# Gate/up products from the first 128 rows on, with all gate/up weights resident, loads on two queues and contiguous fold outputs

## The chip, the cores and the metric

The kernel runs on one core of a Trainium2 chip. Such a core has a matrix engine (TensorE, "PE" in the profile, with its weight loads listed apart as "PEld"), a vector engine (VectorE, "DVE"), a scalar engine (ScalarE, "ACT"), a pool engine that does nothing here, and a sync engine ("SP") whose queue starts the transfers between device memory and the core's on-chip memory. Each engine runs its own instructions strictly in the order in which they were written down; engines wait for each other through semaphores. The metric is the time of one execution in microseconds of the device, as a median over runs.

## The reference

The input `x` has 2048 rows of 640 numbers. It is normalised over its rows (layer norm), and three things are added: `x` itself, a spectral filter A and a gated product B of the normalised rows.

```python
def _A_ref(x, w_r, w_i):
    X = rfft2(x.astype(float32), axes=(-2, -1))
    X = X * (w_r + 1j * w_i)
    return irfft2(X, s=(S, D), axes=(-2, -1)).astype(bfloat16)

def _B_ref(x, w_gate, w_up, w_down):
    g = einsum("bsd,df->bsf", x, w_gate)      # 640 -> 1536
    u = einsum("bsd,df->bsf", x, w_up)        # 640 -> 1536
    return einsum("bsf,fd->bsd", g * u, w_down)   # 1536 -> 640

xn = _layernorm(x)
return x + _A_ref(xn, A_w_r, A_w_i) + _B_ref(xn, B_w_gate, B_w_up, B_w_down)
```

## The kernel before

The 2048 rows are held as 16 blocks of 128. All work is cut into tasks, each a handful of instructions on one engine, with a name that is used below:

- **Normalisation of block b** (DVE): two `bn_stats` (L716, L717), `bn_aggr` (L722), subtract the mean (L744), add epsilon (L729), a square root on ACT (L733), the reciprocal (L737) and the multiplication (L749). Blocks are handled in groups (`_LN_GROUPS`): two single ones, then pairs.
- **T0_b** (PE, L757): five transposes that bring the normalised block into the tile `XT`, whose copy out of PSUM runs on ACT or DVE (`eT0`, L671 or L672).
- **GU** (PE, L836): the gate and up products of one of 12 column groups `ft` of 128 columns with one stretch of 256 rows: ten products of 128x256 into one PSUM bank. `eG` (L671) copies the bank to the small ring `GBF` (three slots), and `H` (DVE, L851) multiplies gate by up into `HT`. There are 96 such units.
- **L1_b, L2_b** (DVE, L778/L779 and L788/L789): a block's row is folded twice, so that the transform over the 640 columns can run on quarters of it. L1 makes sum and difference of mirrored halves, L2 folds those once more into `F`. L2 writes every fourth element, since the four quarters lie interleaved in `F` (`p (r d g) -> p r g d`).
- **R_b** (PE, L798): five products on the folded block; `eR` copies them to `U`, on ACT.
- **D_t, C_t, WM_t, CB_t, IA_t, IB_t** for 16 values t: the transform over columns and rows (PE, L881/L885 and L906 to L909), the multiplication with the filter (DVE, L920, with its combination L929/L930) and the first inverse products (PE, L939, L956). The filter rows for t are loaded into a ring of four slots `W`.
- **I_a, U1_a, U2_a** for 16 blocks a: the rest of the inverse transform (PE L979/L983, ACT, DVE L998/L999 and L1006/L1007).
- **ACC_a_h** (PE, L1024/L1026): 12 products with `w_down` and one with the inverse transform for half of an output block, 32 in all; `FIN` (DVE, L1033) adds `x`, and SP stores the half block.

The order on each engine comes from a planner, `_Sched.plan` (L151). It simulates the engines with a duration for each task, a fixed delay between engines and a simple model of the transfers, and at each step takes, among the tasks whose inputs are planned, the one that can start first, with a preference for low `prio` numbers within a slack. What it writes down is fixed: at run time an engine that waits for one task does not go on to the next. Idle PE time up to `filler_deadline` is planned with dummy products (`fill`, L687/L688), and 56 more of them (`warm`, L698) open the program.

The gate and up weights have 12 column groups, of which the tile `GW` holds eight (`_NGW = 8`). GU therefore runs in two passes (`_FT_GROUPS`): first groups 0 to 7 over all eight stretches of 256 rows, then groups 8 to 11 over all of them, whose weights are loaded into the slots of groups 0 to 3 when the last product on those is done. All transfers are started by SP.

Of the kernel before, what the change touches and what calls it, by code (L numbers as in the profile page):

```python
# [10 lines left out]
_XLAT = 130.0  # L11
_SLAT = {"pe": 0.0, "act": 70.0, "dve": 70.0, "pool": 100.0, "sp": 0.0}
_DMA_BW = 300.0
_DMA_LAT = 1900.0
_DMA_ISSUE = 60.0
# [53 lines left out]
class _Sched(object):  # L69
# [81 lines left out]
    def plan(self, nbanks=8, filler_deadline=0.0):  # L151
# [56 lines left out]
        while nsch < ntot:  # L208
            cands = []
            for t in avail:  # L210
                unit_choice = None
                bank_ready = 0.0
                if t.bank is not None:
# [8 lines left out]
                    if bank_ready > 0.0:  # L222
                        bank_ready += _XLAT
                best = None
                for ei, e in enumerate(t.engs):
                    est = eng_free[e]
                    for d in t.deps:
                        lat = _SLAT[e] if d.eng == e else _XLAT
# [52 lines left out]
            if e == "sp" and t.nbytes:  # L281
                issue_end = est + _DMA_ISSUE
                ds = max(issue_end, dma_pipe)
# [4 lines left out]
            else:  # L288
                t.end = fin
                eng_free[e] = fin  # L290
            seq[e] += 1
# [40 lines left out]
    def compute_waits(self):  # L332
        allt = sorted(self.tasks, key=lambda t: (t.start, t.tid))
        cnt = {}
        for t in self.order["sp"]:
# [8 lines left out]
        def dim_of(d):  # L344
            if d.eng == "sp" and d.nbytes:
# [3 lines left out]
        for t in allt:  # L349
# [3 lines left out]
            for d in deps:  # L353
                dm, val = dim_of(d)
                if d.eng == t.eng and t.eng in ("pe", "sp") and not (d.eng == "sp" and d.nbytes):
                    if known.get(dm, 0) < val:
                        pass
# [35 lines left out]
def _build_tables():  # L393
# [32 lines left out]
    for g in range(4):  # L426
        fd[:, g * 160:(g + 1) * 160] = full[g][0:128]
        fd[g:128:4, 640 + g * 160:640 + (g + 1) * 160] = full[g][128:160]
# [79 lines left out]
def _d_dve_psum(n):  # L508
    return n * 1.04 + 65.0


def _d_dve_psum16(n):
    return n * 0.52 + 65.0


def _d_dve_tt16(n):
    return n * 0.52 + 68.0


def _d_dve_ts16(n):  # L520
    return n * 0.26 + 125.0


def _d_act(n):
    return n * 0.833 + 200.0
# [8 lines left out]
def _build(nc, A_x, A_w_r, A_w_i, B_w_gate, B_w_up, B_w_down, out, opts=None):  # L534
# [3 lines left out]
    with es:  # L538
# [35 lines left out]
        b_gbf = alloc("GBF", 3 * 512)  # L574
# [44 lines left out]
        v_gbf = V("GBF").rearrange("p (r n) -> p r n", r=3)  # L619
        v_dum = V("DUM")  # L620
        v_l = V("L").bitcast(_F32).rearrange("p (r c d) -> p r c d", r=2, c=2)
        v_f = V("F").rearrange("p (r d g) -> p r g d", r=3, g=4)
        v_ff = V("F").rearrange("p (r n) -> p r n", r=3)
        v_a = V("A").rearrange("p (r n) -> p r n", r=3)
# [38 lines left out]
        def dma(name, dst, src, nbytes, writes, prio, semkey=None, reads=(), after=()):  # L663
            def em(c):
                return c.e.dma_start(dst, src)  # L665
            return T(name, "sp", _DMA_ISSUE, em, reads=reads, writes=writes, prio=prio, nbytes=nbytes,
# [456 lines left out]
```

## Time and profile before

| what | us |
|---|---|
| median of the three runs shown | 233.66 |
| lowest and highest of them | 231.93, 234.84 |
| the profiled execution | 232.76 |
| its span, from first to last instruction | 231.0 |

The span is what the views of the trace count from; the 1.8 us between it and the execution's own time lie around it. The profiled execution stands 0.90 us below the median. The granted clock of the matrix engine is 1.000 throughout.

A group's row gives busy time, mean duration and the idle time ahead of it. A product's duration runs from when it enters the matrix engine to when its last result is out, and products overlap; so a product of 128x256 is listed with 273 ns although the next one starts some 110 ns after it. What a product costs is therefore read from the distance of starts in the view in order of time, and a short wait can hide behind the end of the product before it.

The program has four stretches that can be told apart in the profile: normalisation and transposes (to about 42 us), folds and R (to about 88), the filter with D to IB (to about 133), and the inverse and the output with I and ACC (to the end). GU units are spread over all four, as work that fits between.

### The profile page before, as it was taken

The numbers are of one execution on the slowest core, as the hardware profiler recorded it, in microseconds if no ns is written. First come the engines' busy times: TensorE is split into PE (matmuls) and PEld (weight loads), VectorE is DVE, ScalarE is ACT, GpSimd is POOL, SyncE is SP. The second block draws the span as 40 slices with busy tenths as digits, with TensorE's granted clock in tenths as the row PEclk, the third lists the DMA queues.
The fourth block names the chain that finished last, engine by engine and source line by source line (L and its number), as shares of the span: only waits on it lengthen the run. The fifth ranks groups of instructions, "written<-read, shape, count | busy, mean of one in ns | idle before, by whom it ended". The sixth has DMA issues, their size and how long they took to land.

```text
span 231.0 us, 4957 instructions
## 1 busy us (share of the span) xinstructions
PE 220.2 (95%) x2002; PEld 180.8 (78%) x2002; DVE 170.3 (74%) x461; ACT 106.6 (46%) x194; POOL 0.2 (0%) x4
## 2 busy tenths in 40 slices
PE   8899999999999999998998998999999999999985
PEld 8789989977777778877876887777777887877753
DVE  4988999999999995999999769899962222222221
ACT  2356565766666667775775665223200230303010
POOL 0000000000000000000000000000000000000000
DMA  6999940000000000292232095112223302121101
GB/s 171 373 384 418 366 84 3 1 3 1 3 0 3 0 0 3 58 278 57 64 61 59 3 267 187 31 44 61 57 82 91 99 0 74 43 76 40 52 21 43
DMA packets 19559, 21.14 MB, mean 92 GB/s; under 512 B 2128, under 2 KB 18128, under 8 KB 19408
## 3 DMA queue, kind: packets, MB, share of 16 engines
q1 hardware_dynamic: 19536, 20.82, 29.3%
q8 instruction: 16, 0.26, 0.5%
q14 instruction: 7, 0.06, 0.1%
HBM read 18.19 MB, written 2.62 MB: 90 GB/s over the span
## 4 chain that ended last, share of the span: by engine, by line
PE 59%; DVE 23%; DMA 9%; issue 4%; SPq 3%; ACT 1%
PE ps L836 25%; PE ps L1024 23%; DVE arena L789 5%; DMA arena<-in_B_w_down_dram 4%; DVE arena L920 4%; DVE arena L779 3%; DMA arena<-in_A_w_i_dram 3%; DVE arena L851 3%; SPq L665 3%; DVE arena L788 2%; PE ps L1026 2%; PE ps L757 2%; DVE arena L778 2%; DMA arena<-in_A_x_dram 1%; DVE arena L930 1%
## 5 line engine op out<-in xcount | busy, mean ns | idle before, releaser
L671 ACT ACTIVATE arena<-ps 128x512 bf16<-128x512 f32 (+4 forms) x184 | 103.8, 589 | 106.9 <-PE ps L836 81.9
L836 PE MATMUL ps<-arena 128*128 128x256 bf16 x960 | 112.7, 273 | 1.2 <-issue 1.2
L836 PEld LDWEIGHTS ps<-arena 128*128 128x128 bf16 x960 | 92.3, 98 | 12.3 <-issue 1.5
L1024 PE MATMUL ps<-arena 128*128 128x320 bf16 x384 | 56.9, 299 | 1.8 <-DVE arena L851 1.1
L1024 PEld LDWEIGHTS ps<-arena 128*128 128x128 bf16 x384 | 37.1, 98 | 16.0 <-issue 1.4
L851 DVE TENSOR_TENSOR arena<-arena 128x256 bf16<-128x256 bf16 x96 | 28.5, 297 | 22.5 <-ACT arena L671 22.3
L1033 DVE TENSOR_TENSOR arena<-ps,arena 128x320 bf16<-128x320 f32 x32 | 15.7, 489 | 29.0 <-PE ps L1026 29.0
L920 DVE TENSOR_TENSOR arena<-ps,arena 128x644 f32<-128x644 f32 x32 | 24.9, 821 | 1.3 <-PE ps L909 1.3
L789 DVE TENSOR_TENSOR arena<-arena 128x320 bf16<-128x320 f32 x16 | 15.1, 942 | 0.0
L788 DVE TENSOR_TENSOR arena<-arena 128x320 bf16<-128x320 f32 x16 | 14.2, 886 | 0.0
L779 DVE TENSOR_TENSOR arena<-arena 128x160 f32<-128x160 bf16 x32 | 10.7, 335 | 0.0
L778 DVE TENSOR_TENSOR arena<-arena 128x160 f32<-128x160 bf16 x32 | 10.6, 332 | 0.0
L939 PE MATMUL ps<-arena 128*128 128x256 bf16 x64 | 9.6, 272 | 0.3 <-ACT arena L671 0.3
L1026 PE MATMUL ps<-arena 128*128 128x320 bf16 x32 | 9.6, 299 | 0.0
L716 DVE BATCH_NORM_STATS2 arena<-arena 128x6 f32<-128x320 bf16 x16 | 7.7, 480 | 2.4 <-DMA arena<-in_A_x_dram 2.4
L798 PEld LDWEIGHTS ps<-arena 128*128 128x128 bf16 x80 | 4.9, 113 | 5.8 <-DVE arena L789 5.7
L983 PE MATMUL ps<-arena 128*128 128x160 bf16 x64 | 9.3, 231 | 0.0
L979 PE MATMUL ps<-arena 66*128 66x320 bf16 x32 | 9.2, 300 | 0.0
L798 PE MATMUL ps<-arena 128*128 128x128 bf16 x80 | 7.5, 224 | 1.9 <-DVE arena L789 0.5
L885 PE MATMUL ps<-arena 128*128 128x160 bf16 x64 | 9.1, 233 | 0.0
L881 PE MATMUL ps<-arena 128*128 128x320 bf16 x32 | 9.1, 299 | 0.0
L929 DVE TENSOR_TENSOR arena<-arena 128x322 bf16<-128x322 f32 x16 | 7.8, 491 | 0.2
(46 smaller groups left out, 169.6 us busy)
## 6 DMA issues: line engine op xcount, KB each, us to landing
arena<-in_A_x_dram SPq DMA_DIRECT2D x18, 160.0 KB, 2.3
out_dram<-arena SPq DMA_DIRECT2D x32, 80.0 KB, 1.6
arena<-c_ti SPq DMA_DIRECT2D x1, 2048.0 KB, 19.0
arena<-in_B_w_gate_dram SPq DMA_DIRECT2D x3, 640.0 KB, 5.9
arena<-in_B_w_up_dram SPq DMA_DIRECT2D x3, 640.0 KB, 7.3
arena<-in_A_x_dram SPq DMA_DIRECT2D x3, 640.0 KB, 10.3
arena<-in_B_w_down_dram SPq DMA_DIRECT2D x1, 1920.0 KB, 9.7
arena<-c_tf SPq DMA_DIRECT2D x4, 384.0 KB, 11.8
```

The source lines that it names most:

```text
L671: return c.e.activation(dst, src, _ACTF.Copy)
L778: c.e.tensor_tensor(v_l[:, lr, k, 0:160], v_x[:, b, 0:160], v_x[:, b, 639:479:-1], op)
L779: ins = c.e.tensor_tensor(v_l[:, lr, k, 160:320], v_x[:, b, 319:159:-1], v_x[:, b, 320:480], op)
L788: c.e.tensor_tensor(v_f[:, fr, 0:4:3, :], c0, c1, _OP.add)
L789: return c.e.tensor_tensor(v_f[:, fr, 1:3, :], c0, c1, _OP.subtract)
L798: ins = c.e.matmul(psflat[:, bk * 512 + j * 128: bk * 512 + (j + 1) * 128], st, v_sm[:, 1, :], start=True, stop=True)
L836: ins = c.e.matmul(ps[:, bk, w * 256:(w + 1) * 256], v_gw[:, w, j, r, :], v_xt[:, j, c8 * 256:(c8 + 1) * 256], start=(j == 0), stop=(j == 4))
L851: return c.e.tensor_tensor(v_ht[:, ft, c8 * 256:(c8 + 1) * 256], v_gbf[:, rr, 0:256], v_gbf[:, rr, 256:512], _OP.mult)
L920: ins = c.e.tensor_tensor(v_p[:, r2, w, :, :].rearrange("p c (m e) -> p c e m", e=2), x4, wv, _OP.mult)
L1024: c.e.matmul(ps[:, bk, 0:320], v_ht[:, ft, a * 128:(a + 1) * 128], v_wd[:, ft, sl3], start=(ft == 0), stop=False)
L1026: return c.e.matmul(ps[:, bk, 0:320], v_sm[:, 2, :], v_v[:, a, sl3], start=False, stop=True)
L1033: return c.e.tensor_tensor(v_out[:, a % 2, sl3], ps[:, bk, 0:320], v_xr[:, xs, sl3], _OP.add)
```

## The change

1. **All weights resident.** `_NGW` becomes 12, so no slot of `GW` is loaded twice, and GU is one pass over all 12 groups. The weights come in five pairs of loads (`_GW_LOADS`: column groups 0-1, 2-3, 4-5, 6-7, 8-11), the first four with 512 bytes in a row instead of 1024.
2. **GU in order of arrival.** The stretches (`_CHUNKS`) are 128 rows for the first four blocks and 256 after that: 48 units of ten 128x128 products and 72 of ten 128x256 products, 1200 products instead of 960, in an order sorted by when weights and rows are there. `GBF` gets six slots instead of three. The first four blocks are normalised one by one, and the loads of x are cut to 1, 1, 1, 1, 4 and 8 blocks.
3. **Two queues.** The constants `SM` and the up weights of the first three pairs are started by ACT, ahead of its table load; all else stays on SP.
4. **Folds.** L1 is two operations of 320 columns instead of four of 160. L2 writes contiguously: the quarters lie one after the other in `F`, in a part of 128 and one of 32 columns each, so L2 is two operations of 256 and two of 64 columns. The table `fd` is permuted to match. L1_b is held back until block b+6 is normalised.
5. **The planner's figures** (delays, durations, transfers) are new, and the dummy products end at 7 us of its own time instead of 24.

```diff
-_XLAT = 130.0
-_SLAT = {"pe": 0.0, "act": 70.0, "dve": 70.0, "pool": 100.0, "sp": 0.0}
+_XLAT = {"pe": 140.0, "act": 40.0, "dve": 40.0, "pool": 60.0, "sp": 40.0}
+_SLAT = {"pe": 0.0, "act": 30.0, "dve": 30.0, "pool": 60.0, "sp": 0.0}
+_TAIL = {"pe": 165.0, "act": 90.0, "dve": 90.0, "pool": 100.0, "sp": 0.0}
...
-_X_LOADS = ((0, 1), (1, 1), (2, 2), (4, 4), (8, 4), (12, 4))
-_LN_GROUPS = ((0, 1), (1, 1), (2, 2), (4, 2), (6, 2), (8, 2), (10, 2), (12, 2), (14, 2))
-_NGW = 8
+_X_LOADS = ((0, 1), (1, 1), (2, 1), (3, 1), (4, 4), (8, 8))
+_LN_GROUPS = ((0, 1), (1, 1), (2, 1), (3, 1), (4, 2), (6, 2), (8, 2), (10, 2), (12, 2), (14, 2))
+_NGW = 12
...
-_FT_GROUPS = ((0, 1, 2, 3, 4, 5, 6, 7), (8, 9, 10, 11))
+_GW_LOADS = ((0, 2), (2, 2), (4, 2), (6, 2), (8, 4))
+_CHUNKS = ((0, 1), (1, 1), (2, 1), (3, 1), (4, 2), (6, 2), (8, 2), (10, 2), (12, 2), (14, 2))
...
-        dma("ld_sm", V("SM"), d_sm.rearrange("p t n -> p (t n)"), 128 * 768, [(b_sm, None)], prio=0.005)
+        dma("ld_sm", V("SM"), d_sm.rearrange("p t n -> p (t n)"), 128 * 768, [(b_sm, None)], prio=0.002, q="act")
...
+            def em_l1(c, b=b, lr=lr):
+                c.e.tensor_tensor(v_l[:, lr, 0, :], v_x[:, b, 0:320], v_x[:, b, 639:319:-1], _OP.add)
+                return c.e.tensor_tensor(v_l[:, lr, 1, :], v_x[:, b, 0:320], v_x[:, b, 639:319:-1], _OP.subtract)
...
+                for v_, lo, n in ((v_fm, 0, 128), (v_fr, 128, 32)):
+                    c0 = v_l[:, lr, :, lo:lo + n]
+                    c1 = v_l[:, lr, :, 319 - lo:319 - lo - n:-1]
+                    c.e.tensor_tensor(v_[:, fr, 0:4:3, :], c0, c1, _OP.add)
+                    ins = c.e.tensor_tensor(v_[:, fr, 1:3, :], c0, c1, _OP.subtract)
...
+        for i, (f0, nf) in enumerate(_GW_LOADS):
+            for w_ in range(2):
+                dma("ld_gw%d_%d" % (f0, w_), v_gw[:, w_, :, f0:f0 + nf, :].rearrange("p j r f -> p j (r f)"),
+                    gvs[w_][:, :, f0 * 128:(f0 + nf) * 128], 5 * 128 * nf * 256,
+                    [(b_gw, ("s", w_ * _NGW + f0, w_ * _NGW + f0 + nf))], prio=(0.004, 0.012, 0.022, 0.032, 0.05)[i] + 0.001 * w_,
+                    q="act" if w_ and i < 3 else "sp")
+        w_at = [6.0 + 2.2 * min(ft // 2, 4) for ft in range(12)]
+        c_at = [6.3 + 2.2 * (b0 + nb - 1) for b0, nb in _CHUNKS]
+        units = sorted((max(c_at[ci], w_at[ft]), ci, ft) for ci in range(len(_CHUNKS)) for ft in range(12))
...
-        sch.plan(8, filler_deadline=opts.get("fill_deadline", 24000.0))
+        sch.plan(8, filler_deadline=opts.get("fill_deadline", 7000.0))
```

Three places show what the new order is. First the matrix engine near the start, from the first GU on. In the kernel before (L757 is T0, L836 GU, L687/L688 the dummies):

```order
L836 MATMUL ps<-arena 128x256 [waits q_act,d_16,d_15]
L836 MATMUL ps<-arena 128x256 x19
L757 MATMUL ps<-arena 128x128 [waits q_dve,q_act]
L757 MATMUL ps<-arena 128x128 x4
L757 MATMUL ps<-arena 128x128 [waits q_dve]
...
L836 MATMUL ps<-arena 128x256 x10
L836 MATMUL ps<-arena 128x256 [waits q_dve]
L836 MATMUL ps<-arena 128x256 x9
L687 MATMUL ps<-arena 128x128
L688 MATMUL ps<-arena 128x128
```

And in the changed kernel, where L764 is T0 and L844 GU (the `d_` names are the semaphores of single loads: `d_3` and `d_4` those of the first pair of weights, `d_5` and `d_6` of the second):

```order
L764 MATMUL ps<-arena 128x128 [waits q_dve,d_0]
L764 MATMUL ps<-arena 128x128 x4
L693 MATMUL ps<-arena 128x128
L694 MATMUL ps<-arena 128x128
...
L844 MATMUL ps<-arena 128x128 [waits q_act,d_4,d_3]
L844 MATMUL ps<-arena 128x128 x19
L764 MATMUL ps<-arena 128x128 [waits q_dve,q_act]
...
L844 MATMUL ps<-arena 128x128 [waits d_6,d_5]
L844 MATMUL ps<-arena 128x128 x19
L844 MATMUL ps<-arena 128x128 [waits q_act]
```

GU now follows the first T0 (with ten pairs of L693/L694 between them) and needs one block and one pair of weights, where it stood behind two T0 and needed two blocks; the dummies after the first four units are gone. (Rows that only repeat are not shown.)

Second, what SP starts first. Before:

```order
L665 DMA arena<-in_A_x_dram 128x640
L665 DMA arena<-c_sm 128x384
...
L665 DMA arena<-in_A_x_dram 128x1280
L665 DMA arena<-in_B_w_gate_dram 128x5x512
L665 DMA arena<-in_B_w_up_dram 128x5x512
L665 DMA arena<-in_A_x_dram 128x2560
...
L665 DMA arena<-in_A_x_dram 128x2560 x2
L665 DMA arena<-c_fd 128x1280
```

And now, on SP (ACT has `c_sm` and three up loads of 128x5x256 as its first four instructions, ahead of its table load):

```order
L671 DMA arena<-in_A_x_dram 128x640
L671 DMA arena<-in_B_w_gate_dram 128x5x256
...
L671 DMA arena<-in_B_w_up_dram 128x5x256
L671 DMA arena<-in_A_x_dram 128x2560
L671 DMA arena<-in_B_w_gate_dram 128x5x512
L671 DMA arena<-in_B_w_up_dram 128x5x512
L671 DMA arena<-in_A_x_dram 128x5120
L671 DMA arena<-c_fd 128x1280
```

Single blocks of x and gate loads alternate four times at the top of the new list, so the second half of x (128x5120) is the last thing ahead of the tables; and the pair of gate/up loads that stood between the filter loads later on is gone from SP.

Third, the matrix engine near the end. Before (L1024/L1026 is ACC, each on a half block):

```order
L1024 MATMUL ps<-arena 128x320 x11
L1026 MATMUL ps<-arena 128x320
L836 MATMUL ps<-arena 128x256 [waits q_dve]
L836 MATMUL ps<-arena 128x256 x9
L1024 MATMUL ps<-arena 128x320 [waits q_dve,d_29,d_19]
```

And now (L844 is GU, L985/L989 is I, L1030/L1032 is ACC), from the last GU on; behind the last row here come two more I and then nothing but ACC:

```order
L844 MATMUL ps<-arena 128x256 x10
L985 MATMUL ps<-arena 128x320 [waits q_dve]
L989 MATMUL ps<-arena 128x160 x2
L985 MATMUL ps<-arena 128x320
L989 MATMUL ps<-arena 128x160 x2
L1030 MATMUL ps<-arena 128x320 [waits d_33,d_24]
L1030 MATMUL ps<-arena 128x320 x11
L1032 MATMUL ps<-arena 128x320
```

The last 16 GU units stood between the ACCs, in groups of six, four, four and two; now the last GU stands ahead of the first ACC, and the last 31 ACCs follow one another to the end.

More of the change, by code (lines that the diff above doesn't have):

```diff
@@ L227, in plan @@
                     for d in t.deps:
-                        lat = _SLAT[e] if d.eng == e else _XLAT
+                        lat = _SLAT[e] if d.eng == e and not d.nbytes else _XLAT[e]
                         de = d.end + lat
@@ L334, in compute_waits @@
         cnt = {}
-        for t in self.order["sp"]:
+        for t in self.order["sp"] + self.order["act"]:
             if t.nbytes:
@@ L344, in dim_of @@
         def dim_of(d):
-            if d.eng == "sp" and d.nbytes:
+            if d.nbytes:
                 return ("dma", d.semkey), d.semval
```

209 lines of the change are left out of this document (96 added, 113 removed).

## Prediction

> **What bounds the kernel now.** I read the page's first two parts, then stretches of time, then the matrix engine in order of time, and last the waits and the chain.
>
> ```profile
> PE 220.2 (95%) x2002; PEld 180.8 (78%) x2002; DVE 170.3 (74%) x461; ACT 106.6 (46%) x194; POOL 0.2 (0%) x4
> ...
> 10.00:42.00 32.00, 31.18 (x319) 28.04 (x320) 29.30 (x105) 18.67 (x35) 0.00 (x0) 1.00 0.70 244
> 42.00:85.50 43.50, 41.66 (x401) 34.46 (x398) 43.29 (x128) 29.58 (x50) 0.00 (x0) 1.00 0.01 2
> 104.00:133.00 29.00, 27.43 (x243) 22.70 (x244) 26.62 (x52) 18.80 (x39) 0.00 (x0) 1.00 0.23 49
> ```
>
> The columns of the last three rows are the stretch, its length, and the busy time of PE, PEld, DVE, ACT and POOL, then clock, transfer share and GB/s. PE is the bound, with DVE full beside it from 42 to 85.5 us (43.29 of 43.50). Time can be saved only where PE waits, idles or works for nothing. The start, as the engines have it:
>
> ```profile
> 1.05 5.00 PE L698 MATMUL ps<-arena 128*128 128x128 bf16 x56 [1.05 <-DVE arena L705]
> 3.06 0.49 DVE L716 BATCH_NORM_STATS2 arena<-arena 128x6 f32<-128x320 bf16 x1 [2.03 <-DMA arena<-in_A_x_dram]
> 3.06 0.53 SPq L665 DMA_DIRECT2D arena<-in_B_w_up_dram  x1
> 4.71 0.20 ACT L733 ACTIVATE arena<-arena 128x1 bf16<-128x1 bf16 x1 [2.70 <-DVE arena L729]
> 6.09 0.33 DVE L749 TENSOR_SCALAR arena<-arena 128x640 bf16<-128x640 bf16 x1
> 6.57 0.44 PE L757 MATMUL ps<-arena 128*128 128x128 bf16 x5 [0.30 <-DVE arena L749]
> 7.05 0.70 ACT L671 ACTIVATE arena<-ps 128x640 bf16<-128x640 bf16 x1
> 10.41 2.34 PE L836 MATMUL ps<-arena 128*128 128x256 bf16 x20 [0.77 <-issue]
> 12.59 0.72 PE L757 MATMUL ps<-arena 128*128 128x128 bf16 x10
> 13.15 2.35 PE L836 MATMUL ps<-arena 128*128 128x256 bf16 x20
> 15.33 0.22 PE L687 MATMUL ps<-arena 128*128 128x128 bf16 x1
> ...
> 16.57 3.44 PE L836 MATMUL ps<-arena 128*128 128x256 bf16 x30 [0.41 <-issue]
> ```
>
> The first GU starts at 10.41 us; up to there PE did two T0 (0.56 us by the ten of 12.59 to 13.15) and 9.85 us of nothing useful. From 15.33 to 16.57 there are dummies again, 1.24 us. In the fold stretch, PE and DVE stand thus:
>
> ```profile
> 49.65 0.47 PE L798 MATMUL ps<-arena 128*128 128x128 bf16 x5 [0.49 <-DVE arena L789]
> 49.96 2.35 PE L836 MATMUL ps<-arena 128*128 128x256 bf16 x20
> ...
> 85.51 0.47 PE L798 MATMUL ps<-arena 128*128 128x128 bf16 x5
> ...
> PEld ps L798 <- DVE arena L789: 5.7, 14, 0.8
> ...
> 60.39 0.34 DVE L851 TENSOR_TENSOR arena<-arena 128x256 bf16<-128x256 bf16 x1
> 60.63 0.33 DVE L778 TENSOR_TENSOR arena<-arena 128x160 f32<-128x160 bf16 x1
> ...
> 61.57 0.30 DVE L851 TENSOR_TENSOR arena<-arena 128x256 bf16<-128x256 bf16 x1
> 61.77 0.89 DVE L788 TENSOR_TENSOR arena<-arena 128x320 bf16<-128x320 f32 x1
> 62.43 0.94 DVE L789 TENSOR_TENSOR arena<-arena 128x320 bf16<-128x320 f32 x1
> 63.15 0.34 DVE L851 TENSOR_TENSOR arena<-arena 128x256 bf16<-128x256 bf16 x1
> ```
>
> 13 rounds of one R and two GU take 35.86 us, 2.76 each. Weight loads for R wait 5.7 us for L2 in 14 places; the products' row hides most of that. One DVE round (60.39 to 63.15, also 2.76) is H 0.24, L1 0.94, H 0.20, L2 0.66 and 0.72. DVE sets this stretch's pace. Later PE waits are few:
>
> ```profile
> PE ps L906 <- DMA arena<-in_A_w_i_dram: 1.7, 3, 0.9
> PE ps L1024 <- DVE arena L851: 1.1, 1, 1.1
> PE ps L1024 <- DMA arena<-in_B_w_down_dram: 0.7, 1, 0.7
> PE ps L939 <- ACT arena L671: 0.3, 1, 0.3
> ```
>
> And the price of the products, and the end:
>
> ```profile
> 181.21 6.71 PE L836 MATMUL ps<-arena 128*128 128x256 bf16 x60
> 187.76 1.79 PE L1024 MATMUL ps<-arena 128*128 128x320 bf16 x12
> ...
> 226.59 1.63 PE ps L1024 x12
> 228.39 0.49 DVE arena L1033
> ```
>
> 60 products of 256 columns take 6.55 us, 109.2 ns each. The last ACC starts at about 226.5 us and 2.6 us follow its end (228.39 to 231.0); that tail stays.
>
> **The change, part by part.** The sum is made against the profiled execution, 232.76 us, which stands 0.90 below the median.
>
> *First GU.* It needs one block now. Block 0's chain keeps its length, bounded below by the rows: statistics at 3.06, square root done at 4.91, then a reciprocal and 0.33 of multiplication, so ready by 5.4 if block 1 no longer stands between (in the new order it does not). But PE runs its 56 opening dummies until about 6.05, so T0_0 comes at about 6.1 to 6.5, its copy takes 0.70 behind 0.44, and the ten pairs of dummies written behind T0_0 (20 by 56 ns, 1.1 us) end at about 7.5. GU starts at 7.5 with 0.28 us of T0 done: 7.2 lost instead of 9.85, minus 2.6. Bounds: minus 3.0 (no dummy delays) and minus 1.2 (weights late, next).
>
> *Loads.* How fast the narrower weight rows come, no row shows. These bound it:
>
> ```profile
> 5.00:9.00 4.00, 3.70 (x67) 3.56 (x65) 3.95 (x15) 1.24 (x3) 0.00 (x0) 1.00 1.05 343
> ...
> 18.00:21.00 3.00, 3.00 (x35) 2.75 (x33) 2.48 (x9) 2.01 (x4) 0.00 (x0) 1.00 1.03 400
> ```
>
> From 5 to 9 us the 1024-byte rows of the weights move, with all 16 transfer engines full (1.05): 327 GB/s, 50 ns a row. From 18 to 21 the 3072-byte rows of `c_tf`: 388 GB/s, 127 ns. A straight line gives 31 ns for 512 bytes, 264 GB/s. The lower end is the filter's 642-byte rows, 49 GB/s at a share of 0.23, so 213 GB/s and 48 ns; at 48 ns, 512 bytes make 170 GB/s. The upper end is 327. I take the line, between sizes that were measured. Since the engines are full with one queue issuing, the second queue adds no rate. Then the first pair (with x block 0 and `SM` ahead, 0.92 MB from 2.0 us on) lands at 5.2 to 5.8, ahead of 7.5. Block 1, with 1.3 MB ahead of it over both queues, lands at about 6.6, against 5.05 before, and its T0 is ready 2.3 us later, at 9.0, while PE has two GU (20 products, 1.1 us) until 8.6: a new wait of 0.4. T0_2 and T0_3 I give 0.2 each, because DVE has block 3's statistics ahead of block 2's multiplication. So 0.8 of new waits for 1.24 of dummies and waits that go: minus 0.4; bounds minus 1.2 and plus 2.5 (pairs at 170 GB/s).
>
> *The second half of x* is now the last load: 0.75 MB of small loads at 327, 2.62 of narrow weights at 264, 1.31 of wide ones at 327, 1.97 of wide x at 388 make 21.3, so it lands at 23.3 us (21.4 to 28.8 by the bounds). Queued behind it on DVE are eight normalisations, with H between, and two folds, ahead of the first R; the 10-to-42 row has 29.30 us of DVE for 14 blocks with their H, so 16.7 for eight, and 3.5 for the folds: 43.5. PE reaches that R at 7.2 + 0.8 + 38.0 (16 T0 of 0.28, 480 products at 56 ns, 60 at 109.2) = 46.0. Cover 2.5 us; cost 0, and one for one beyond.
>
> *Narrow products.* 240 products of 256 columns become 480 of 128. T0 has the shape with a weight load each, 56 ns: 26.9 against 26.2, plus 0.7. R's 61 to 62 ns (49.65 to 49.96) would make plus 3.3, the upper end; the lower is 0. I take T0, whose weights lie contiguously as GU's do; R's were interleaved. ACT's 24 and DVE's 24 more copies and H (a fixed part of some 0.15 and 0.08 us each) lie beside PE: ACT was busy 18.67 of 32 us. If DVE were not covered, H's part would be 1.9 us.
>
> *Folds.* L1 and L2 with contiguous writes I price by rows of the chain that read f32 and write contiguous bf16, 322 columns:
>
> ```profile
> 112.37 0.50 DVE arena L929
> 112.87 0.40 DVE arena L930
> 113.27 1.48 DVE arena L920 x2
> ```
>
> About 0.40 each, 1.04 ns a column and some 0.07 fixed. L1 becomes 2 by 0.40, L2 2 by 0.34 and 2 by 0.135: 1.75 against 2.32, and a DVE round 2.76 − 0.57 = 2.19. A PE round needs 20 by 109.2 ns and R's 0.28: 2.46. So PE leads, and what is late next is PE's own work. Saved: 13 by (2.76 − 2.46) = 3.9, and the first wait's 0.49: minus 4.3. If instead the four-fold reading order cost what the writing did, L2 would stay at 1.4 and the round at 2.65: minus 1.5, the other end.
>
> *Filter stretch.* Filter rows wait no more behind a pair of weight loads on SP. Five GU more stand here (18, by the order, against 13): 5.5 us more PE work and 1.1 more DVE, where DVE was busy 26.62 of 29 and PE 27.43, so PE leads here too. Of the waits of 1.7 and 0.3 I let 0.6 stay (a ring of four is refilled by four starts of about half a microsecond on SP): minus 1.4; bounds 0 and minus 2.0.
>
> *Inverse and output.* The load of `w_down` starts when IB is done. By the order PE now has 14 I and 19 GU between that and the first ACC, against five I and six GU with a wait of 0.7, so the 0.7 goes. With no GU among the ACCs the 1.1 for H goes. 31 ACCs in a row are new as a count, not as a kind: minus 1.8.
>
> The sum: −2.6 − 0.4 + 0.7 − 4.3 − 1.4 − 1.8 = −9.8. From 232.76 that is 223.0; from the median 223.9.
>
> A rule of the Trainium skill weighs against the narrow products: the page "TensorE: Matmul & The Clock Gate", section "Back-to-back issue gap", says that in a stream in which each product has its own weight load, both set the distance, and gives about 81 ns at 128 columns. As an estimate from that figure, 480 by 25 ns more would cost 12 us and the change would come out at 236. Here T0's ten run at 56 ns with ten weight loads, so the trace does not bear it out for that line.
>
> **Rivals.**
>
> *Weight loads come out.* In GU the loads could cease to hide behind products of half the length.
>
> ```profile
> L836 PEld LDWEIGHTS ps<-arena 128*128 128x128 bf16 x960 | 92.3, 98 | 12.3 <-issue 1.5 <-ACT arena L671 0.5
> ```
>
> A load takes 98 ns; if each of the 480 narrow products had to wait for its own, that is 480 by 42 ns, 20.2 us, and 244.1 in all: slower. It eats the whole gain from 76 ns a product on. For it: PEld's 98 exceeds 56. Against: T0 and the dummies have the same row and run at 56. The Trainium skill's rule above speaks of this mechanism. Chance 0.04.
>
> *The loads are the bound.* At 170 GB/s the second half of x lands at 28.8, DVE reaches the first fold at 49.0, and PE loses 3.0; the early pairs cost some of the same time before. 223.9 + 3.0 = 226.9, up to 230 if two queues hinder each other. For it: 512-byte rows are half of what was measured. Chance 0.15.
>
> *DVE keeps the fold stretch.* Mirrored f32 reading in L2 is not in the trace; at the other end of that term, 223.9 + 2.8 = 226.7. Chance 0.07.
>
> *The gain is given back.* If PE arrives earlier at the filter stretch and finds DVE there as the bound, the fold's 4.3 returns as waits: 228.2, within 2%. For it: DVE at 26.62 of 29. Against: five GU more. Chance 0.06.
>
> **How the numbers follow.** The forecast itself has 0.68 and, by the spread of its own terms, 221 to 226. The range must leave out at most 0.2: I go from 219.5 (all lower ends of the small terms, minus 2.5, and the run-to-run spread of 1.7) to 229. 2% of 233.66, about what a measurement of this kernel can tell from no change, is 4.7: the border is 229.0. Faster: 0.68, the folds' 0.07 and 0.12 of the loads' 0.15: 0.87. Same: 0.03 and 0.06, 0.09. Slower: 0.04.
>
> **What would show it.** In the changed profile the first GU should start near 7.5 us, T0_1 wait a few tenths, rounds of R and two GU take 2.46 us with DVE idle in them, L2's four operations be near 0.42 and 0.22 us long each, no filter-row wait exceed half a microsecond, and the last 31 ACCs be evenly spaced by 1.77. Narrow GU with starts over 60 ns apart, DVE waiting on x at the second half, or waits of GU for H (six ring slots give about 2 us) would make it wrong.

## The result and the profile after

| | before | after |
|---|---|---|
| median of the runs | 232.80 us (231.66 to 234.84) | 223.67 us (223.59 to 223.76) |
| profiled execution | 232.76 us | 223.76 us, span 221.8 |
| ratio of the times | | 0.960, 95% interval 0.952 to 0.968 |
| start of the last product on PE | 228.06 us | 218.91 us |

Faster, by 9.1 us; the four runs before were taken beside the four after. One execution of the experiment `b` below, the one that was profiled, took 616.43 us for a reason that stays open, so `b` is read from its other three and from the same kernel's second run, `b2`.

PE's share has gone from 95 to 98% of the span, and DVE's busy time has fallen by 8.1 us, as the page of the changed kernel says (engines; then the costliest groups with busy time and mean ns of one):

```profile
PE 216.7 (98%) x2204; PEld 184.3 (83%) x2204; DVE 162.2 (73%) x481; ACT 112.0 (50%) x225; POOL 0.2 (0%) x4
...
L844 PE MATMUL ps<-arena 128*128 128x256 bf16 (+1 forms) x1200 | 115.5, 251 | 0.6 <-ACT arena L677 0.5
...
L796 DVE TENSOR_TENSOR arena<-arena 128x256 bf16<-128x256 f32 (+1 forms) x32 | 10.2, 318 | 0.0
L797 DVE TENSOR_TENSOR arena<-arena 128x256 bf16<-128x256 f32 (+1 forms) x32 | 10.2, 317 | 0.0
```

L844 is GU, L796 and L797 are the fold L2. The start of the changed kernel in order of time:

```profile
1.05 5.57 PE L704 MATMUL ps<-arena 128*128 128x128 bf16 x56 [1.05 <-DVE arena L711]
...
3.66 0.49 DVE L723 BATCH_NORM_STATS2 arena<-arena 128x6 f32<-128x320 bf16 x1 [2.63 <-DMA arena<-in_A_x_dram]
...
5.75 0.39 DVE L756 TENSOR_SCALAR arena<-arena 128x640 bf16<-128x640 bf16 x1
...
6.45 0.44 PE L764 MATMUL ps<-arena 128*128 128x128 bf16 x5
...
6.93 0.70 ACT L677 ACTIVATE arena<-ps 128x640 bf16<-128x640 bf16 x1 [1.41 <-PE ps L764]
...
7.85 1.28 PE L844 MATMUL ps<-arena 128*128 128x128 bf16 x20
```

The first GU starts at 7.85 us instead of 10.41. Block 0 of `x` is used 0.6 us later than before (3.66 against 3.06), with `SM` now moving beside it.

The loads came at the rate that the prediction drew between two measured ones. From 5 to 9 us, where mostly rows of 512 bytes move, the window reads (the same columns as in the prediction's first fence):

```profile
5.00:9.00 4.00, 4.00 (x66) 3.95 (x64) 2.93 (x11) 1.50 (x4) 0.00 (x0) 1.00 1.15 302
```

302 GB/s at a share of 1.15 make 263 GB/s, 31 ns a row, where the straight line had 264. The second half of `x` is started at 11.84 us and lands 11.9 later, at 23.7, against 23.3 in the prediction; the first R waits for nothing. So the rival that the loads are the bound did not come true.

The fold stretch, first its window (the third stretch of the prediction's first fence, in the same columns), then two rounds of it:

```profile
42.00:85.50 43.50, 43.50 (x445) 39.48 (x443) 40.04 (x140) 31.89 (x56) 0.00 (x0) 1.00 0.01 2
...
53.09 0.44 PE L807 MATMUL ps<-arena 128*128 128x128 bf16 x5
53.36 2.35 PE L844 MATMUL ps<-arena 128*128 128x256 bf16 x20
...
54.12 0.42 DVE L796 TENSOR_TENSOR arena<-arena 128x256 bf16<-128x256 f32 x1
54.46 0.42 DVE L797 TENSOR_TENSOR arena<-arena 128x256 bf16<-128x256 f32 x1
54.79 0.22 DVE L796 TENSOR_TENSOR arena<-arena 128x64 bf16<-128x64 f32 x1
54.93 0.22 DVE L797 TENSOR_TENSOR arena<-arena 128x64 bf16<-128x64 f32 x1
...
55.55 0.44 PE L807 MATMUL ps<-arena 128*128 128x128 bf16 x5
```

From one R (L807) to the next is 2.46 us, PE is busy throughout, and DVE, which was full before, has 3.5 us to spare. The filter stretch, and PE's only row from there on in the list of waits:

```profile
104.00:133.00 29.00, 29.00 (x265) 25.20 (x264) 24.86 (x51) 20.83 (x41) 0.00 (x0) 1.00 0.24 55
...
PE ps L985 <- DVE arena L1013: 0.6, 2, 0.5
```

Nothing waits for filter rows or `w_down` any more. New are two waits of I (L985) for U2. What PE loses early, in the one place where it is most, reads thus:

```profile
16.86 0.49 DVE L723 BATCH_NORM_STATS2 arena<-arena 128x6 f32<-128x320 bf16 x1 [1.22 <-DMA arena<-in_A_x_dram]
...
20.04 0.20 ACT L740 ACTIVATE arena<-arena 128x2 bf16<-128x2 bf16 x1 [0.70 <-DVE arena L736]
20.15 0.64 ACT L677 ACTIVATE arena<-ps 128x256 bf16<-128x256 f32 x2
...
20.66 0.72 PE L844 MATMUL ps<-arena 128*128 128x128 bf16 x10 [0.54 <-ACT arena L677]
```

Blocks 4 to 7 of `x` land together, so block 4's statistics start at 16.86; in the kernel before they started at 12.54. The square root for blocks 4 and 5 stands on ACT ahead of a GU's copy and waits 0.70 us for DVE; PE waits for that copy.

To compare kernels I measured, between the starts of each two products in a row on PE, what goes beyond the steady distance of that shape (55.6 ns at 128 columns, 109.2 at 256, and so on). This is called PE's loss below. By stretch, from the first GU on:

| loss, us | first GU to 45 us | 45 to 91 (folds) | 91 to 135 (filter) | 135 on |
|---|---|---|---|---|
| before | 0.71 (1.38 with dummies) | 4.54 | 3.07 | 2.32 |
| after | 2.62 | 0.20 | 0 | 1.15 |

### The profile page after: what moved, and what is told of

It is laid out like the page before. It is cut to its first block, busy times and chain, and to the rows that moved or that the text cites. A ratio compares the mean times of both kernels' runs of the same rounds, so it can differ in the third digit from the quotient of the medians.

```text
span 221.8 us, 5449 instructions
## 1 busy us (share of the span) xinstructions
PE 216.7 (98%) x2204; PEld 184.3 (83%) x2204; DVE 162.2 (73%) x481; ACT 112.0 (50%) x225; POOL 0.2 (0%) x4
## 3 DMA queue, kind: packets, MB, share of 16 engines
q10 hardware_dynamic: 2112, 1.08, 1.9%
HBM read 18.19 MB, written 2.62 MB: 94 GB/s over the span
## 4 chain that ended last, share of the span: by engine, by line
PE 87%; DMA 4%; DVE 3%; SPq 3%; issue 1%; ACT 0%
PE ps L844 43%; PE ps L1030 23%; DMA arena<-in_A_x_dram 4%; PE ps L945 3%; SPq L671 3%; PE ps L807 2%; PE ps L891 2%; PE ps L887 2%; PE ps L1032 2%; PE ps L985 2%; PE ps L989 2%; PE ps L764 2%; PE ps L962 2%; PE ps L913 1%; PE ps L914 1%; PE ps L912 1%
## 5 line engine op out<-in xcount | busy, mean ns | idle before, releaser
L677 ACT ACTIVATE arena<-ps 128x512 bf16<-128x512 f32 (+5 forms) x214 | 109.3, 543 | 47.0 <-PE ps L844 37.7
L844 PE MATMUL ps<-arena 128*128 128x256 bf16 (+1 forms) x1200 | 115.5, 251 | 0.6 <-ACT arena L677 0.5
L844 PEld LDWEIGHTS ps<-arena 128*128 128x128 bf16 x1200 | 96.1, 98 | 9.1 <-issue 0.7
L1030 PE MATMUL ps<-arena 128*128 128x320 bf16 x384 | 56.6, 299 | 0.0
L1030 PEld LDWEIGHTS ps<-arena 128*128 128x128 bf16 x384 | 37.5, 98 | 14.5
L859 DVE TENSOR_TENSOR arena<-arena 128x256 bf16<-128x256 bf16 (+1 forms) x120 | 30.9, 258 | 11.9 <-ACT arena L677 9.6
L796 DVE TENSOR_TENSOR arena<-arena 128x256 bf16<-128x256 f32 (+1 forms) x32 | 10.2, 318 | 0.0
L797 DVE TENSOR_TENSOR arena<-arena 128x256 bf16<-128x256 f32 (+1 forms) x32 | 10.2, 317 | 0.0
L985 PE MATMUL ps<-arena 66*128 66x320 bf16 x32 | 9.3, 301 | 0.6 <-DVE arena L1013 0.6
L945 PE MATMUL ps<-arena 128*128 128x256 bf16 x64 | 9.6, 273 | 0.0
L1032 PE MATMUL ps<-arena 128*128 128x320 bf16 x32 | 9.6, 299 | 0.0
L989 PE MATMUL ps<-arena 128*128 128x160 bf16 x64 | 9.3, 231 | 0.0
L1004 DVE TENSOR_TENSOR arena<-ps,arena 128x320 f32<-128x320 f32 x16 | 7.8, 485 | 0.3
L935 DVE TENSOR_TENSOR arena<-arena 128x322 bf16<-128x322 f32 x16 | 7.8, 487 | 0.1
L1012 DVE TENSOR_TENSOR arena<-arena 128x320 bf16<-128x320 f32 x16 | 7.7, 484 | 0.1
L936 DVE TENSOR_TENSOR arena<-arena 128x322 bf16<-128x322 f32 x16 | 7.8, 486 | 0.0
L786 DVE TENSOR_TENSOR arena<-arena 128x320 f32<-128x320 bf16 x16 | 7.7, 483 | 0.0
```

What stands on the lines that cost most here:

```text
L677: return c.e.activation(dst, src, _ACTF.Copy)
L844: ins = c.e.matmul(ps[:, bk, w * n:(w + 1) * n], v_gw[:, w, j, ft, :], v_xt[:, j, rows], start=(j == 0), stop=(j == 4))
L859: return c.e.tensor_tensor(v_ht[:, ft, rows], v_gbf[:, rr, 0:n], v_gbf[:, rr, n:2 * n], _OP.mult)
L945: ins = c.e.matmul(ps[:, bk, lt * 256:(lt + 1) * 256], v_y[:, r2, cc, lt:256:2], v_ti[:, t, cc, :], start=(cc == 0), stop=(cc == 1))
L985: c.e.matmul(ps[:, bk + h, 0:320], v_z2[0:66, 2, h, a, :], v_g[0:66, 640 + 320 * h: 960 + 320 * h], start=True, stop=False)
L989: ins = c.e.matmul(ps[:, bk + h, e * 160:(e + 1) * 160], v_z2[:, e, h, a, :], v_g[:, g * 160:(g + 1) * 160], start=False, stop=(e == 1))
```

## The experiments

Times are medians of the runs; each kernel was timed beside the kernel before, whose medians in those sets were 232.6 to 233.1 us.

**The folds alone**, put into the kernel before (`a`), and taken out of the changed one (`b`, and the same kernel once more as `b2`, whose trace is used). The edit, as a diff of the kernel before for `a`, and the other way round for `b`:

```diff
...
-        v_f = V("F").rearrange("p (r d g) -> p r g d", r=3, g=4)
...
+        v_fm = v_ff[:, :, 0:512].rearrange("p r (g d) -> p r g d", g=4)
+        v_fr = v_ff[:, :, 512:640].rearrange("p r (g d) -> p r g d", g=4)
...
-                    c0 = v_l[:, lr, :, 0:160]
-                    c1 = v_l[:, lr, :, 160:320]
...
+                        c0 = v_l[:, lr, :, lo:lo + n]
+                        c1 = v_l[:, lr, :, 319 - lo:319 - lo - n:-1]
...
```

> The kernel before, with nothing changed but the four fold lines: L1 and L2 write contiguous tiles, and the weight operand of R is read contiguously. Instruction order on all engines as before. Theory: the fold stretch loses its 0.3 us a round, 13 rounds, and R's first wait: 4 to 4.5 us of the 9.1 come from here alone, so about 228.3 (227.5 to 229.5). The four fold operations read 0.4 and about 0.22 us, a round of R and two GU 2.46. Rival (the gain is given back later): PE reaches the filter stretch earlier and waits there for DVE or for the filter's rows, and the time stays at 231 or above.

> The changed kernel with the old, interleaved fold outputs; instruction order as in the changed kernel. Theory: DVE sets the fold stretch again, a round is 2.76 instead of 2.46, and the time is 223.7 + 4 to 4.5 = about 228. Rival (the rest of the change carries the fold stretch, because its H are spread otherwise): no more than 1 us slower, 224.7 or less.

> The changed kernel with the old, interleaved fold outputs once more, for its trace: it came out 5.7 us slower, where the old folds' rounds explain 4 to 4.5. Theory: the rounds stand at 2.76 and make 4 to 4.5, and the other 1.2 to 1.7 us stand behind the last fold, where DVE comes late to the filter stretch with H it has not done (loss there over 1 us against 0.17). Rival: all of it is in the fold stretch, in rounds of 2.85 or more or in more than 14 of them.

`a`: 228.38 us, ratio 0.979 (0.972 to 0.985), so 4.3 us come from the folds alone. Its loss from 45 to 91 us is 0.12, and its filter stretch loses 2.90 where the kernel before lost 3.07: nothing was given back. The fold window of `a`, beside the one above:

```profile
42.00:85.50 43.50, 43.50 (x447) 39.36 (x445) 37.92 (x130) 31.86 (x55) 0.00 (x0) 1.00 0.01 2
```

`b`: 229.39 us, 5.7 above the changed kernel, more than I had allowed for. `b2` (229.37) shows the old rounds, L2 with 0.89 and 0.94 us in L797 and L798, and R's weight load waiting for it:

```profile
57.92 0.47 PE L807 MATMUL ps<-arena 128*128 128x128 bf16 x5
...
59.02 0.89 DVE L797 TENSOR_TENSOR arena<-arena 128x320 bf16<-128x320 f32 x1
59.69 0.94 DVE L798 TENSOR_TENSOR arena<-arena 128x320 bf16<-128x320 f32 x1
...
60.68 0.30 PEld L807 LDWEIGHTS ps<-arena 128*128 128x128 bf16 x5 [0.39 <-DVE arena L798]
60.68 0.47 PE L807 MATMUL ps<-arena 128*128 128x128 bf16 x5
```

Each round is 2.76 us. The rest of the 5.7 is in the fold stretch too, so the rival of that run holds and my theory fell: PE waits ahead of 16 R (14 in the kernel before), once for 1.08 us, and the loss there is 5.63 against 0.15 in the filter stretch. In the kernel before, the first two R stand between T0, at 42.4 and 46.5 us, and wait for nothing; here all sixteen stand behind the last T0, the first at 48.2, and every one goes at DVE's pace. The folds are worth 4.3 us in the old kernel and 5.7 in the new.

**The planner's figures**: the old ones in the changed kernel (`c`), the new ones in the kernel before (`h`). The edit as a diff for `c`:

```diff
...
-_XLAT = {"pe": 140.0, "act": 40.0, "dve": 40.0, "pool": 60.0, "sp": 40.0}
...
-_TAIL = {"pe": 165.0, "act": 90.0, "dve": 90.0, "pool": 100.0, "sp": 0.0}
+_XLAT = {"pe": 130.0, "act": 130.0, "dve": 130.0, "pool": 130.0, "sp": 130.0}
...
+_TAIL = {"pe": 0.0, "act": 0.0, "dve": 0.0, "pool": 0.0, "sp": 0.0}
...
-_DMA_ISSUE = 440.0
...
+_DMA_ISSUE = 60.0
...
```

> The changed kernel with the planner's latencies and durations of before (the due time of the fills stays). Only the order changes. Theory: the filter stretch's lost 2.85 us came from the filter's rows no longer queueing behind a pair of weight loads and from more GU standing there, not from the new figures, so the time stays within 1.5 us of 223.7. Rival: the new figures place DVE's and PE's work so that waits vanish, and without them the filter stretch and the end lose 3 us again: 227 or more.

> The kernel before (two passes of weights, one queue, wide first chunks, old fold outputs) with only the planner's new figures and costs. Theory: the filter row's wait of about 1.1 us behind the pair of weight loads, the wait for w_down and the one for H at the end need the resident weights to go, so no more than 1 us is gained against before: 231 to 234. Rival: the figures alone remove these waits, 2 to 4 us faster: 229 to 231.

`c`: 224.62 us, inside the theory's bounds, but its trace speaks against the theory. The filter stretch loses 1.81 us again, in waits of 0.1 to 0.5, most of them ahead of IA (L945) and one of 0.30 for a filter row, and only because I's waits at the end are gone (0.17 against 1.15) does the total come out within a microsecond. `h`: 230.55 us, ratio 0.992 (0.988 to 0.995), so the figures alone are worth some 2 us: inside the rival's bounds, at their small end, and more than the theory's 1. The wait for `w_down` is gone, as the rival had it. But one wait of 0.91 us for a filter row stays in the filter stretch, and it is nearly all that is lost there; the wait for H ahead of the last ACCs (1.27) stays too:

```profile
PE ps L1028 <- DVE arena L855: 1.1, 1, 1.1
...
PE ps L910 <- DMA arena<-in_A_w_i_dram: 0.7, 1, 0.7
```

So the filter stretch's 3.07 us were of three kinds, by the distances between starts. The wait for a row behind the second pass of the weights, 1.09 us, stays with the new figures (`h`) and goes with the resident weights. Two more waits for rows, 0.35 and 0.71, are gone in `h`, and `c` has one of 0.30. The waits of PE for copies and other short ones, some 0.9, go with the planner's figures and are back in `c`.

**One queue** for all loads (`d`):

```diff
-            return T(name, q, _DMA_ISSUE, em, reads=reads, writes=writes, prio=prio, nbytes=nbytes,
+            return T(name, "sp", _DMA_ISSUE, em, reads=reads, writes=writes, prio=prio, nbytes=nbytes,
```

> The changed kernel with every load issued by SP, none by ACT. Theory: the transfer engines are what the loads wait for, so one queue issues as fast as they can take it: within 0.7 us of 223.7, with x block 0 landing near 3.06 again because SM no longer moves beside it. Rival: SP's issues block when its queue is full (2.7 us at a time), blocks 1 to 7 of x come later, and the start loses 2 us: 225.7 or more.

223.59 us, no difference. Block 0 is used at 3.11 us instead of 3.66 and the first GU starts at 7.45, but block 1 comes later, and its T0 with it:

```profile
7.06 0.49 DVE L723 BATCH_NORM_STATS2 arena<-arena 128x6 f32<-128x320 bf16 x1 [1.47 <-DMA arena<-in_A_x_dram]
...
9.68 0.44 PE L764 MATMUL ps<-arena 128*128 128x128 bf16 x5 [0.95 <-DVE arena L756]
```

What one queue gains in front (0.4 us) it loses behind (3.40 us lost up to 45 us, against 2.62), and 0.5 of I's waits go besides. So the times are equal in part by the luck of the order near the end; the early part alone is 0.4 us worse with one queue.

**The width of the chunks and of the weight loads**: all chunks of 256 rows (`e`), all of 128 (`f`), three pairs of four weight groups (`g`).

```diff
-_CHUNKS = ((0, 1), (1, 1), (2, 1), (3, 1), (4, 2), (6, 2), (8, 2), (10, 2), (12, 2), (14, 2))
+_CHUNKS = tuple((2 * i, 2) for i in range(8))      (e)
+_CHUNKS = tuple((i, 1) for i in range(16))         (f)
-_GW_LOADS = ((0, 2), (2, 2), (4, 2), (6, 2), (8, 4))
+_GW_LOADS = ((0, 4), (4, 4), (8, 4))               (g)
```

> The changed kernel with GU in eight chunks of 256 rows, so that the first GU needs two blocks of x, T0 and copies. Theory: GU starts about 1.5 to 2 us later, the narrow products' 0.5 us comes back: 224.7 to 225.5. Rival: the pieces of the start overlap anyway and the waits for blocks 1 to 3 go too, so the time is 223.7 or less.

> The changed kernel with GU in sixteen chunks of 128 rows throughout: 720 products of 256 columns become 1440 of 128. Theory: each stands at 55.6 ns, its weight load hidden: 720 x (2 x 55.6 - 109.2) = 1.4 us on PE, and DVE's extra H (36 x 0.08 = 2.9 us) and ACT's copies lie beside it except in the fold stretch, where a round now has 2 H more (0.16): 225 to 226. Rival (weight loads come out when there are many in a row): at 81 ns each +38 us, at the load's own 98 ns +62.

> The changed kernel with the gate and up weights loaded in three pairs of four instead of four pairs of two and one of four (1024-byte rows in place of 512). Theory: the rows move at 50 ns per 1024 bytes against 31 per 512, a fifth less transfer time for the first 2.6 MB, but the first pair is twice as large and lands about 2.3 us later, after the first GU would start at 7.85: one wait of about 1 to 2 us ahead of it, and less waiting later: 224 to 225.5. Rival (narrow rows cost the early waits): the 2.4 us of early waits mostly go, and the time is 223 or less.

`e`: 222.85 us, the rival. The first GU starts at 10.63, as late as in the kernel before, and still the kernel is no slower; three of its four runs (222.53 to 223.10) lie below all runs of the changed one, while the fourth is the profiled one, of 224.23. There 16 products from 11.5 us on stood twice as far apart (1.66 us); without them next to nothing is lost from the first GU to 45 us, against 2.62. The early start is given back in full within the first 40 us.

`g`: 226.23 us, worse than the theory's number and the rival's. GU starts at 8.43, and then PE waits ahead of the T0 of blocks 1 to 3 (0.8, 0.3 and 0.8 us) and twice behind a T0 (0.5 us, for weights, and 1.0): 4.72 us lost up to 45 us. Rows twice as wide did not pay for pairs twice as large.

`f`: 229.36 us, 5.7 above the changed kernel, where the theory had 1.4. In the profiled execution, of 230.26 us, PE's loss is over 5 us above the changed kernel's. After the first GU, 38 waits of 0.06 to 0.10 us make 3.0 and nine of 0.10 to 0.15 make 1.2. Nearly all of the 38 stand between GU and GU. Seven of the nine stand ahead of R and wait for L2, as the last two rows below show: L2 ends at 61.16 and R starts at 61.21. DVE has more to do than the expectation counted, for 192 GU units instead of 120 make 72 more H and not 36. ACT's copies eG between two folds show the rhythm of the 38:

```profile
58.86 0.38 ACT L677 ACTIVATE arena<-ps 128x256 bf16<-128x256 f32 x1 [0.17 <-PE ps L844]
...
59.42 0.38 ACT L677 ACTIVATE arena<-ps 128x256 bf16<-128x256 f32 x1 [0.17 <-PE ps L844]
...
60.07 0.38 ACT L677 ACTIVATE arena<-ps 128x256 bf16<-128x256 f32 x1 [0.27 <-PE ps L844]
...
60.63 0.38 ACT L677 ACTIVATE arena<-ps 128x256 bf16<-128x256 f32 x1 [0.18 <-PE ps L844]
...
60.94 0.22 DVE L797 TENSOR_TENSOR arena<-arena 128x64 bf16<-128x64 f32 x1
...
61.21 0.45 PE L807 MATMUL ps<-arena 128*128 128x128 bf16 x5
```

The copies start 0.56, then 0.65, then 0.56 us apart: two GU take 1.21 us instead of the 1.11 of 20 products. The planner lets GU alternate between two PSUM banks (it prefers a bank whose partner is in use). A bank is filled in 0.56 us, its copy starts 0.20 later (at 58.86, where the first product of the next GU started at 58.66) and takes 0.38, and between 52 and 76 us each GU product that came late by 0.08 started 0.055 to 0.057 us after a copy's end. Together that is 1.19 for a turn that 20 products would make in 1.11, and the difference is the 0.08. Two experiments try this. In `i`, the narrow kernel, eG copies only the gate half:

```diff
-                return copy_on(c, v_gbf[:, rr, 0:2 * n], ps[:, bank_of(gu), 0:2 * n])
+                return copy_on(c, v_gbf[:, rr, 0:n], ps[:, bank_of(gu), 0:n])
...
-                return c.e.tensor_tensor(v_ht[:, ft, rows], v_gbf[:, rr, 0:n], v_gbf[:, rr, n:2 * n], _OP.mult)
+                return c.e.tensor_tensor(v_ht[:, ft, rows], v_gbf[:, rr, 0:n], v_gbf[:, rr, 0:n], _OP.mult)
```

> The run with sixteen narrow chunks, but eG copies only the gate half of its bank to SBUF and H multiplies that half by itself: the copy of the up half is left out. Instruction order unchanged. Theory: in the narrow run, the 38 waits of 0.08 us and the nine of 0.10 to 0.15 end a constant 0.055 us after ACT's copy of the bank that the GU is to write; with the shorter copy (some 0.26 us for 0.38) they vanish and 3 to 4.5 us of 229.4 go: 225 to 226.5. Rival (weight loads or the issue of narrow products cause them): they stay, 229 to 229.5.

226.77 us, 2.6 below `f` and a little above my number. The copy group of `f` and of `i` in the listing by shape, one after the other:

```profile
L677 ACT ACTIVATE arena<-ps 128x256 bf16<-128x256 f32 x192 | 73.2, 383 | 26.9 <-PE ps L844 22.5
```

```profile
L677 ACT ACTIVATE arena<-ps 128x128 bf16<-128x128 f32 x192 | 53.0, 277 | 37.2 <-PE ps L844 35.6
...
PEld ps L807 <- DVE arena L797: 1.5, 7, 0.2
```

With 277 ns instead of 383, five of the 38 waits are left, with the same 1920 products and weight loads. So neither weight loads nor the issue of narrow products made them. What did not go is in the last row: R waits for L2 in seven places, 1.5 us. The expectation took these for waits for the copy, but in `f` these R start 0.20 us after a copy's end and 0.05 after L2's; they were seven of 0.14 there and are seven of 0.21 here.

**The choice of the bank** in the changed kernel (`j`), and with it chunks of 128 rows for the first two blocks only (`k`); line numbers are higher by one in both:

```diff
-                    key = (pen, st[0])
+                    late = max(0.0, st[0] + _XLAT["pe"] - eng_free["pe"])
+                    key = (late, pen, st[0])
...
-_CHUNKS = ((0, 1), (1, 1), (2, 1), (3, 1), (4, 2), (6, 2), (8, 2), (10, 2), (12, 2), (14, 2))
+_CHUNKS = ((0, 1), (1, 1), (2, 2), (4, 2), (6, 2), (8, 2), (10, 2), (12, 2), (14, 2))      (k)
```

> The changed kernel with one line of the planner different: among single PSUM banks it prefers one that is free when PE comes to it, over one that completes a half-used pair, so GU no longer alternates between two banks. Theory: the ten waits of 0.08 us in the narrow chunks go (0.8 us), and since the planner then sees PE running on, a part of the 0.7 at 20 us and of I's 0.97 may go: 221.5 to 223. Rival (the 0.08 is a price of the wait itself, whichever bank is waited for): 223.4 to 223.9, and the ten waits stand as before.

> As the run before, and only the first two chunks are of 128 rows, the other seven of 256. Theory: 240 narrow products fewer give back half of the narrow chunks' 0.48 us, and with fewer pieces ACT and DVE have less to do per product while x arrives; GU still starts near 7.85: 221 to 222.3, the fastest of all. Rival (the first products of the 256-row chunk of blocks 2 and 3 wait for both blocks, 0.5 to 1.5 us): 222.5 to 224.

`j`: 221.93 us, ratio 0.955 (0.950 to 0.959); of the ten short waits up to 45 us one is left, and the loss there falls from 2.62 to 1.13 us. Since the planner orders the tasks anew, the loss of I (0.65 from 135 us on) and of the wait at 20 us differ too; not all of the 1.7 us is the short waits'. `k`: 220.34 us, ratio 0.947 (0.943 to 0.950), the fastest of all, 3.3 us below the changed kernel and below my bounds. The list of waits names one of PE after its opening:

```profile
7.77 1.28 PE L845 MATMUL ps<-arena 128*128 128x128 bf16 x20
...
PE ps L765 <- DVE arena L757: 0.2, 1, 0.2
```

GU starts at 7.77, 0.62 us are lost up to 45 and 0.14 from 135 on. Of the rival's wait for blocks 2 and 3 there is 0.34 us. Now the early start pays: against `e` it begins 2.9 us earlier and, by the starts and losses of the two profiled executions, keeps some 1.7 of that; another 0.5 is the waits of I that `e` has and `k` has not.

## Why the prediction was right, and which of its steps were not

The time was right within 0.3 us, the sign and the range too. Some of that closeness is luck: the median before came out at 232.80 and not at 233.66, and the change was forecast at 9.8 us and measured at 9.1. The sum stands thus against the two profiled executions (loss of PE as defined above; the parts add up to the 9.15 us by which the last product starts earlier, and the tail after it stayed at 2.9):

| term | predicted | measured |
|---|---|---|
| first GU | −2.6 | −2.3 |
| loads and early waits | −0.4 | +1.2 |
| narrow products | +0.7 | +0.5 |
| folds | −4.3 | −4.3 |
| filter stretch | −1.4 | −3.1 |
| inverse and output | −1.8 | −1.2 |
| sum | −9.8 | −9.2 |

*First GU.* The mechanism is as told: opening dummies, T0_0, its copy, dummies behind it. GU starts at 7.85 and not at 7.5, since block 0 came 0.6 us later with `SM` beside it; in `d`, with all loads on one queue, it is 3.11 and 7.45.

*Loads and early waits* is the step that failed. The prediction let the second to fourth blocks wait 0.8 us in all. What PE lost in those places is 0.83, but only 0.51 of it for these blocks (0.38 for block 2, 0.14 for block 3, against 0.4). The T0 of block 1 waited 0.08 us, 0.056 after the end of a GU's copy, so for a bank and not for its data, and the 0.24 behind it are GU waiting for the second pair of weights; so the near sum is luck. And the prediction took the GU between these places to run on by themselves, which left out two things: seven waits of GU for its bank, 0.08 us each and 0.56 in all, and the 0.70 at 20.66 us, where a square root on ACT waits for DVE ahead of a copy. The last section of the prediction names waits of GU for H as what would make it wrong; it was the copy ahead of H. The narrow chunk halves what hides the copy's turn, and this was costed as busy time of ACT and DVE beside PE (18.67 of 32 us), where the turn of one bank decides. With these losses, the narrow first chunks bring nothing: `e` without them is 0.8 us faster.

*Narrow products.* The distance is that of T0, as taken. In order of time in the changed kernel:

```profile
21.94 4.07 PE L844 MATMUL ps<-arena 128*128 128x128 bf16 x70
25.85 0.44 PE L764 MATMUL ps<-arena 128*128 128x128 bf16 x5
```

70 products in 3.91 us are 55.9 ns each, with a weight load each. The 81 ns that the Trainium skill gives ("TensorE: Matmul & The Clock Gate", "Back-to-back issue gap") would be 5.7 us for these 70. `f` with 1920 of them and `i` with the same and a shorter copy leave no room for it either. The 61 to 62 ns of R, the prediction's upper end, were no cost of interleaved weights: behind a wait for L2 the first distance of the five is 81 to 86 ns and the other four are 56, and the first two R of the kernel before, which wait for nothing, run at 56 throughout with the same interleaved weights.

*Folds.* The numbers held: 0.42 us for the long and 0.22 for the short operations, a PE round of 2.46, no waits. DVE is busy for 2.32 us of a round, where the prediction had 2.19. The rival that the gain is given back in the filter stretch is refuted by `a`.

*Filter stretch.* The size was off by 1.7. The prediction priced only the waits that the list of waits names, 1.7 and 0.3 us, and let 0.6 of them stay. PE lost 3.07 us there. By the distances between starts the four waits of the list make 2.6 us and not 2.0, because the modelled ends of the products cover part of each, and the rest are shorter waits, most of 0.08 to 0.15 us, that the list does not show. All went. `h` and `c` divide them: the row behind the weights' second pass, some 1 us, and the figures of the planner for most of the rest. The prediction gave the figures no term at all.

*Inverse and output.* The 0.87 and the 1.27 went, as told, but in the new order I waits for U2 twice, 0.33 and 0.64 us. That the new order sets these I close behind their U2 had no term in the prediction. The orders of `c` and `k` have almost none of it (0.17 and 0.14 lost from 135 us on), so it belongs to this order of tasks and not to the resident weights.

Errors of 1.6 and 1.7 us with opposite signs made the total better than its parts; that too was luck. *The second queue adds no rate* is borne out by `d`: without that queue the start loses 0.4 us, and not the 2 of that run's rival.

## What to carry to other kernels

- When a task is made shorter, look at the turn of its buffers and not only at the busy shares: with two banks, fill, start of the copy, copy and handing back must fit into two tasks (here 1.19 us against 1.11). A share of 58% on ACT said nothing of that; the rhythm of its copies did.
- An earlier start is worth what the next pieces let it keep. Ask for each following piece when its data, its copy and its buffer are there, and compare with a version that starts late but never stops; here that one was faster, until the bank was freed.
- Price waits from the distances between starts on the bound engine, not only from a list of waits: a third of what was lost in the filter stretch was not in the list.

## What the runs showed of the hardware that was not expected

- The granted clock of PE fell to 0.57 in a stretch of the profiled execution of `e`, soon after PE had waited 1.5 us at 7.7 and 1.05 us at 9.5 us. In a window of that run:

```profile
11.00:15.00 4.00, 4.00 (x24) 2.96 (x22) 3.22 (x14) 1.37 (x4) 0.00 (x0) 0.57 1.13 342
```

  The 16 products from 11.5 us on stood about 214 ns apart instead of 109, 1.66 us in all. Two of the other three executions of the same kernel had a mean clock of 1.0, the third 0.999, so this order of instructions alone does not decide it. Four executions of the kernel before have a mean clock of 0.993, and they took 234.39 to 236.36 us. The stretch of 16 times 0.214 us, 3.4 us, has the length that the Trainium skill states for a window of the clock gate ("TensorE: Matmul & The Clock Gate", "Part 1: The HAM clock gate"), after an idle one of which it goes to half. Half is what the distances show, but PE was not idle for a whole window before it: in the 3.4 us up to 11.5 us it ran five products of T0 and eight of GU, 1.2 us of work by their distances. Why the clock fell stays open. Whether more dummies there would help wasn't tried.
- Starting a load takes SP 0.4 to 0.6 us as a rule, but some starts held it for up to 2.7 us. In order of time in the changed kernel:

```profile
4.40 0.43 SPq L671 DMA_DIRECT2D arena<-in_B_w_gate_dram  x1
4.88 2.74 SPq L671 DMA_DIRECT2D arena<-in_B_w_up_dram  x1
7.66 2.60 SPq L671 DMA_DIRECT2D arena<-in_A_x_dram  x1
```

  So blocks 4 to 7 of `x` were not even started before 7.66 us. The transfer engines were full then (a share of 1.15 from 5.0 to 7.6 us), but also from 2 to 5 us (1.03), where starts took 0.4 to 0.5; so full engines alone do not explain it, and the cause stays open.
